# Late mode rows of a spectral mix: from waiting for them in every token tile to adding them by small row-group products in 16 of 36 tiles

## The chip, the cores and the metric

The kernel runs on one core of a Trainium2 chip. The metric is the device time of one execution in microseconds (us). The engines are TensorE (PE, with its weight load PEld), VectorE (DVE), ScalarE (ACT), GpSimd (POOL) and SyncE (SP); SP, ACT and POOL also issue DMAs, each from a queue of its own that it works off in order.

## What is computed

Two stages follow each other. First sliding-window causal attention over `q`, `k`, `v` of shape (8 batches, 8 heads, 576 tokens, 64), with a window of 64 tokens; its output `x` is (8, 576, 512). Then a spectral mix over the tokens:

```python
X = np.fft.rfft(x, axis=1)
Xr, Xi = (np.real(X[:, :n_modes]), np.imag(X[:, :n_modes]))   # 64 modes
Yr = np.einsum('bmd,mde->bme', Xr, w_r) - np.einsum('bmd,mde->bme', Xi, w_i)
Yi = np.einsum('bmd,mde->bme', Xr, w_i) + np.einsum('bmd,mde->bme', Xi, w_r)
Y[:, :n_modes] = Yr + 1j * Yi
y = np.fft.irfft(Y, n=S, axis=1)
u = x + y
return (u + np.maximum(u @ w_ch, 0.0)).astype(np.float32)
```

`w_r` and `w_i` are 64 matrices of 512 x 512 in fp32 (134 MB together, read once), `w_ch` is one.

## The kernel before

**Order of the work.** Attention and the forward transform fill `x_sb`, `x4` (x in bf16) and `XQ` (the transform of x by mode, one tile for each half of the 512 input channels). Meanwhile POOL issues the loads of `w_r` and `w_i` one after the other into rings of buffers (L156); a load converts fp32 to bf16 on the way and waits until the products that read its buffer's former contents are done. The modes are worked off in 16 groups of four (`steps`): `mode_half` (L165 to L182) multiplies four modes for one half of the channels and one of the two weights, with four 32-column groups of the PE array side by side (8 products of 512 columns). I call each such call a half-step. The loads set its pace: 2 loads of 512 KB as written, every 4.97 us. The groups 14 and 15 come before 12 and 13 (`LAST` = 12), so groups 12 and 13 are the last; their 16 rows of the 128-row spectrum (real and imaginary part of eight modes) are the **late rows**.

**What is done between half-steps.** A list `jobs` is worked off by `advance()`, a set number after each half-step. An *x job* makes x w for one token tile (four transposes, ACT copy, four products with `wch` on L591, DVE copy into `XW[i]`). A *batch job* (L654) prepares the spectrum of one batch: DVE copies `YT[:, b]` to fp32 (L657), PE turns it (L660), ACT writes `Yall[:, b]`, PE multiplies by `w_ch`, DVE writes `Zall[:, b]` (L665). `Yall` holds Y and `Zall` holds Y w_ch, each with 128 rows for each batch; batches 0 and 1 have tiles of their own (`Y0`, `Z0`, `Y1`, `Z1`). `advance()` keeps one job in flight: a job's products come after the next job's transposes. The jobs are given out so that 34 of them (26 x jobs, 8 batch jobs) are spread over the 22 half-steps before the last two, and what is left is drained there.

**The end of the loads.** Before the very last half-step, PE gets fillers (`keep_warm`, L186, products that nobody reads: 5 ahead and 4 inside), the sums of the first of the two late groups for batches 0 and 1 (`put_first`) and three products for the first tiles.

**The tail (L798 to L838).** When the last group has been added up, DVE writes it to `stg` (L612). PE turns it (L623), ACT copies it (L636), and then the late rows are made in two ways: for batches 0 and 1 directly by small products into `Y0`, `Y1`, `Z0`, `Z1` (L804, L805, L812, L830), and for all batches through `yst` and `zst`, which two DMAs on SP's queue scatter into the late rows of `Yall` (L815) and `Zall` (L824). Then 36 token tiles of 128 x 512 are finished: 32 of one batch, and 4 (`x4`) that hold the last 64 tokens of two batches. Each tile needs u = x + T Y and r = x w + T Z, and gives u + max(r, 0). Odd tiles ("by DVE", L691) take a product T Y (L697), a product of the identity with `XW` (L723), a product T Z (L697); DVE adds x (L715), ACT takes the maximum (L730), POOL adds (L731). Even tiles take one more product, the identity with x (L703); ACT copies u (L718), DVE does the rest (L733). An x4 tile needs two products T Y and two T Z. Buffers for u come in pairs from a ring of 7; PSUM banks go round in five pools (`m`, `t`, `y`, `p`, `z`). Outputs leave from SP's queue (L738), the last few also from ACT's.

Of the kernel before, what the change touches and what calls it, by code (L numbers as in the profile page):

```python
# [26 lines left out]
def kernel(  # L27
# [36 lines left out]

    consts = pool("consts")
# [4 lines left out]
    pick = consts.tile([128, 2, 24], BF16, name="pick")  # L70
# [12 lines left out]
    XQ = {0: xpool.tile([128, 3 * NJ + 2, B, NM], BF16, name="XQ0")}  # L83
    late = {}
# [80 lines left out]
    def mode_half(psm, grp, hb, ri, first, last):  # L165
        pairs = range(4 * grp, 4 * grp + 4)
        order = [(j, p) for j in range(NJ) for p in pairs]
# [3 lines left out]
        for j, p in order:  # L171
            g = p % 4
            if ending and j == 0 and g >= 2:
                keep_warm(2)
            nc.tensor.matmul(out=psm[32 * g:32 * g + 32, :],  # L175
                             lhsT=XQ[hb].rearrange("k s b m -> k (s b) m")[:, (3 * j + 1 - ri) * B:(3 * j + 5 - ri) * B, p],
# [11 lines left out]
    with tc.manual_schedule():  # L188
# [223 lines left out]
        def trig_steps():  # L412
# [5 lines left out]
            yield lambda: ve.tensor_copy(out=pick[:, :, 8:16], in_=sel.rearrange("p g (r b) -> p b (g r)", b=B)[:, 0:2])  # L418
            yield lambda: zero_xq(1, ve)

# [92 lines left out]
        Y0 = zpool.tile([128, DM], BF16, name="Y0")  # L513
        Z0 = zpool.tile([128, DM], FP32R, name="Z0")
        Y1 = zpool.tile([128, DM], BF16, name="Y1")
        Z1 = zpool.tile([128, DM], FP32R, name="Z1")
        rowpool = pool("rowpool", reuse_waits="tile")
        trpool = pool("trpool", bufs=3, reuse_waits="tile")
# [55 lines left out]

        def yrows(b):
            return (Y0, Y1)[b] if b < 2 else Yall[:, b, :]

        def zrows(b):
            return (Z0, Z1)[b] if b < 2 else Zall[:, b, :]

# [13 lines left out]
        def advance():  # L594
            if jobs:
                prepare, done = jobs.pop(0)
                pend.append((prepare(), done))
                if len(pend) < 2:
                    return
            if pend:  # L600
                tr, done = pend.pop(0)
                done(multiply(tr))
# [4 lines left out]
        def finish_group(grp, psm):  # L607
# [22 lines left out]
            def put_first():  # L630
                for b in range(2):
                    nc.tensor.matmul(out=late["first"][32 * b:32 * b + 16, :], lhsT=pick[:, b, 8 - 8 * i:24 - 8 * i],
                                     rhs=stg, start=(i == 0), stop=(i == 1), tile_position=(0, 32 * b))

            def take():
                nc.scalar.copy(out=late["tr"][:, :, 64 * i:64 * i + 64], in_=pt[:, :, 64 * i:64 * i + 64])  # L636

            def prepare():
                turn()
                if end:  # L640
                    put_y()
                    late["tr"] = Zall[:, 0, :].rearrange("p (c k) -> p c k", c=NDCH)
# [5 lines left out]
            if end:  # L648
                late[i] = turn, put_first, take, put_y
# [4 lines left out]
        def batch_job(b):  # L654
# [9 lines left out]
            def done(pz):  # L664
                nc.vector.tensor_copy(out=zrows(b), in_=pz)  # L665

            jobs.append((prepare, done))

# [9 lines left out]
        def x_jobs(pl, lo, hi):  # L678
            for i in range(lo, hi):
                def done(pz, i=i):  # L680
                    XW[i] = pl.tile([128, DM], FP32R, name=f"xw{i}")
                    nc.vector.tensor_copy(out=XW[i], in_=pz)  # L682
                jobs.append((lambda i=i: transposed(tiles[i][0]), done))

        AHEAD = 4
        pu, us, ps = {}, {}, {}
# [3 lines left out]

        def by_dve(i):  # L691
            return i % 2 == 1 and i < NT - 3
# [7 lines left out]
        def tail_x(i):  # L700
            pu[i] = bank("mmy"[i % 3])
            if not by_dve(i):
                nc.tensor.matmul(out=pu[i].rearrange("p (h e) -> p h e", h=2), lhsT=ident_bf, rhs=tiles[i][0],  # L703
                                 start=True, stop=False)

        def tail_u(i):
            if i < NT:
                if i not in pu:
                    tail_x(i)
                add_rows(pu[i], i, trigI, yrows, by_dve(i))  # L710
                if i % 2 == 0:
                    late["u"] = ringA.tile([128, 2, DM], FP32, name="ut", tag="wt")
                us[i] = late["u"][:, i % 2, :]
                if by_dve(i):
                    nc.vector.tensor_tensor(out=us[i].rearrange("p (h e) -> p h e", h=2),  # L715
                                            in0=pu[i].rearrange("p (h e) -> p h e", h=2), in1=tiles[i][0], op=ALU.add)
# [154 lines left out]
```

## Time and profile before

| what | us |
|---|---|
| three runs, median (lowest to highest) | 441.35 (441.26 to 441.49) |
| the profiled execution, its own time | 441.02 |
| span of its trace | 439.2 |
| start of the last `stg` copy (L612) | 398.01 |
| first output DMA issued (L738) | 403.05 |
| last DVE instruction of the tail (L733) ends | 434.05 |

Span and own time differ by 1.82 us that lie outside the trace. Busy shares over the span: PE 80%, DVE 50%, ACT 40%, POOL 33%. Times in the trace are us from the start of the span. A line of the timeline has start, duration, engine, line, operation, output <- inputs, shape, count, and in brackets how long the engine had been idle and what ended that.

### The profile page before, as it was taken

To read this page: it belongs to the slowest core of one execution; us is meant where nothing else is said; L and a number is where in the kernel's file an instruction comes from. 1 tells how busy PE (TensorE), PEld (TensorE's weight loads), DVE (VectorE), ACT (ScalarE), POOL (GpSimd) and SP (SyncE) were. 2 spreads that over 40 slices of the span, in tenths; PEclk is the share of its full clock that TensorE was granted. 3 is DMA by queue.
4 is the path that set the end of the run, shared out by engine and by line. 5 is a ranking of instruction groups with operands and counts; after the bars stand their busy time and mean duration, and the time that the engine had idled before them with its cause. 6 is when DMAs were issued, how large, how long until landed. Compare 5 with 4: busy or idle time off the path is not lost.

```text
span 439.2 us, 10995 instructions
## 1 busy us (share of the span) xinstructions
PE 350.0 (80%) x4728; PEld 219.5 (50%) x4728; DVE 219.9 (50%) x447; ACT 173.7 (40%) x307; POOL 143.4 (33%) x211
## 2 busy tenths in 40 slices
PE   6999999998999997986336565766778766799994
PEld 3666767676767664662113223334454433453552
DVE  8588787876776763775014111212223122345773
ACT  5666667575667663533002101111122121124662
POOL 9333323323233233223232232122232222301773
PEclk9999999999999996988559556788889689899999
DMA  8999999999999999999999999999999999992887
GB/s 205 211 211 211 212 210 211 211 211 211 212 211 212 212 210 211 211 212 211 211 258 211 211 211 211 211 211 211 212 211 211 211 211 211 212 177 67 271 305 263
DMA packets 47873, 93.45 MB, mean 213 GB/s; under 512 B 3536, under 2 KB 3664, under 8 KB 47824
## 3 DMA queue, kind: packets, MB, share of 16 engines
q0 software_dynamic: 42000, 81.73, 98.6%
q1 hardware_dynamic: 5600, 10.62, 7.2%
q8 instruction: 37, 0.61, 0.5%
q10 hardware_dynamic: 224, 0.39, 0.3%
q14 instruction: 12, 0.10, 0.1%
HBM read 163.58 MB, written 9.44 MB: 394 GB/s over the span
## 4 chain that ended last, share of the span: by engine, by line
DMA 47%; PE 41%; issue 5%; ACT 3%; DVE 3%; POOL 1%; DVEq 0%; POOLq 0%
DMA wi<-in_moe_w_i_dram 24%; DMA wr<-in_moe_w_r_dram 11%; DMA rawk<-in_k_dram 7%; PE tr L222 6%; DMA wch<-in_moe_w_ch_dram 4%; PE s L269 4%; PE pt L289 4%; PE s L261 4%; PE s L281 3%; PE psm L175 3%; PE vb L234 3%; PE o L309 2%; PE psz L591 1%; PE psm L697 1%; PE pst L723 1%
## 5 line engine op out<-in xcount | busy, mean ns | idle before, releaser
L591 PE MATMUL psz<-wch,tr 128*128 128x512 f32 x176 | 67.2, 517 | 10.9 <-DMA wch<-in_moe_w_ch_dram 10.9
L156 POOL DMA_DIRECT2D wi<-in_moe_w_i_dram x62 | 43.9, 709 | 95.7 <-PE psm L175 49.2
L682 DVE CAST xw<-psz 128x512 fp32r<-128x512 f32 x36 | 24.9, 691 | 91.4 <-PE psz L591 90.9
L156 POOL DMA_DIRECT2D wr<-in_moe_w_r_dram x53 | 37.9, 714 | 87.9 <-PE psm L175 38.0
L175 PEld LDWEIGHTS <-XQ 128*32 128x32 bf16 x512 | 24.0, 165 | 81.0 <-issue 73.6
L273 DVE TENSOR_REDUCE mx<-s 128x4 fp32r<-128x512 f32 x72 | 49.5, 687 | 26.3 <-PE s L269 26.0
L568 ACT CAST tr<-ptx 128x512 fp32r<-128x512 bf16 x36 | 21.1, 587 | 103.8 <-PE ptx L584 103.8
L175 PE MATMUL psm<-wi,XQ 128*32 128x512 bf16 x244 | 34.0, 466 | 30.6 <-DMA wi<-in_moe_w_i_dram 30.6
L591 PEld LDWEIGHTS psz<-wch,tr 128*128 128x128 f32 x176 | 40.1, 252 | 17.4 <-issue 11.2
L175 PE MATMUL psm<-wr,XQ 128*32 128x512 bf16 x212 | 29.8, 485 | 22.0 <-DMA wr<-in_moe_w_r_dram 21.3
L283 ACT ACTIVATE p<-s 128x512 bf16<-128x512 f32 x72 | 39.8, 604 | 13.0 <-PE s L281 13.0
L226 ACT COPY kT<-tr 128x576 bf16<-128x576 bf16 x32 | 23.2, 724 | 24.4 <-PE tr L222 24.4
L731 POOL TENSOR_TENSOR ut<-ut,XQ 128x512 f32<-128x512 f32 x16 | 20.5, 1284 | 28.1 <-ACT XQ L730 27.5
L292 DVE COPY pts<-pt 128x1024 bf16<-128x1024 bf16 (+1 forms) x40 | 25.2, 629 | 8.3 <-PE pt L289 7.0
L269 PE MATMUL s<-kT,qT 64*64 64x128 bf16 (+1 forms) x576 | 29.2, 221 | 0.0
L261 PE MATMUL s<-mask_t,ident_bf 128*128 128x512 bf16 x72 | 28.4, 395 | 0.9 <-ACT p L283 0.8
L226 ACT COPY qT<-tr 128x576 bf16<-128x576 bf16 x32 | 23.3, 729 | 10.7 <-PE tr L222 10.7
L269 PEld LDWEIGHTS <-qT 64*64 64x64 bf16 x576 | 17.8, 107 | 18.0 <-issue 17.5
L281 PE MATMUL s<-mx,ident_r 128*128 128x512 f32 x72 | 26.4, 438 | 0.0
L289 PE MATMUL pt<-ident_bf,p 128*128 128x128 bf16 x288 | 23.8, 223 | 1.5 <-issue 1.3
L226 ACT COPY vT<-tr 128x576 bf16<-128x576 bf16 x32 | 23.3, 728 | 4.0 <-PE tr L222 3.9
L321 DVE TENSOR_TENSOR x_sb<-o,r 128x512 bf16<-128x512 f32 x32 | 22.1, 691 | 1.1
(182 smaller groups left out, 567.2 us busy)
## 6 DMA issues: line engine op xcount, KB each, us to landing
wi<-in_moe_w_i_dram POOLq DMA_DIRECT2D x60, 512.0 KB, 15.9
wr<-in_moe_w_r_dram POOLq DMA_DIRECT2D x53, 512.0 KB, 16.3
out_dram<-ut SPq DMA_DIRECT2D x31, 256.0 KB, 2.4
rawv<-in_v_dram POOLq DMA_DIRECT2D x16, 288.0 KB, 14.4
rawk<-in_k_dram POOLq DMA_DIRECT2D x15, 288.0 KB, 15.1
rawq<-in_q_dram POOLq DMA_DIRECT2D x15, 288.0 KB, 14.1
Ypair<-in_moe_w_r_dram POOLq DMA_DIRECT2D x5, 512.0 KB, 14.9
x_sb<-in_moe_w_r_dram POOLq DMA_DIRECT2D x4, 512.0 KB, 15.2
```

The lines of the kernel that those rows point to most:

```text
L156: nc.gpsimd.dma_start(out=w[:, 0:len(ps)], in_=src[ps[0]:ps[-1] + 1, HALF * hb:HALF * hb + HALF, :].rearrange("g (p j) e -> p g j e", j=NJ))
L175: nc.tensor.matmul(out=psm[32 * g:32 * g + 32, :], lhsT=XQ[hb].rearrange("k s b m -> k (s b) m")[:, (3 * j + 1 - ri) * B:(3 * j + 5 - ri) ...
L222: nc.tensor.transpose(out=pt[ro, j, :], in_=raw[ro, TH * half + j, :], identity=ident_bf[ro, ro])
L226: nc.scalar.copy(out=to, in_=pt.rearrange("p j n -> p n j"))
L261: nc.tensor.matmul(out=s, lhsT=ident_bf, rhs=mask_t[:, mk], start=True, stop=True)
L269: nc.tensor.matmul(out=s[ro, t, lo:128], lhsT=lq, rhs=kT[ro, 64 * n - 64 + lo:64 * n + 64], start=False, stop=True, skip_group_check=True)
L273: nc.vector.tensor_reduce(out=mx, in_=s, axis=AX.X, op=ALU.max, negate=True)
L281: nc.tensor.matmul(out=s, lhsT=ident_r, rhs=mx.unsqueeze(2).to_broadcast([128, 4, 128]), start=False, stop=True, skip_group_check=True)
L283: nc.scalar.activation(out=p[:, 4 * c2:4 * c2 + 4, :], in_=s, func=ACT_F.Exp, scale=EX_SCALE)
L289: nc.tensor.transpose(out=pt[:, t, :], in_=st[u]["p"][:, t, :], identity=ident_bf)
L292: nc.vector.tensor_copy(out=ps[:, 0:nt, :], in_=pt[:, 0:nt, :])
L591: nc.tensor.matmul(out=pz, lhsT=tr[:, c, :], rhs=wch[:, c, :], start=(c == 0), stop=(c == NDCH - 1))
```

## The change

Sixteen of the 36 tiles (the four 128-token tiles of each of batches 0 to 3; `NLB` = 4) are handled in two steps.

*Under the last loads* (`early_job`): after the batch job of batch b come four early jobs. Each makes T Z with all rows of `Zall[:, b]` as they are then, the late rows being zero (`trz` and the late rows of `YT` are cleared once), and DVE adds it to `XW[i]` in place; then T Y, to which x is added: for odd c by DVE into a spare region of `XQ`, for even c by one more product (identity with x), copied by ACT over the place of x in `x_sb`. So x + T Y and x w + T Z lack only the late rows. Since `XQ` is overwritten, the columns of the last two groups are copied to `XL` beforehand and `mode_half` reads them there.

*In the tail*: the 16 late rows of batches 0 to 3 are laid on partitions 0, 32, 64 and 96 (`YL`, `ZL`, with matching copies `trigL`, `trigLr` of the late rows of the inverse table, made once by 8 small DMAs). Each of the sixteen tiles takes identity x `XW` and two products over 16 rows in one of four row groups of the array (`late_u`, `late_z`); DVE adds to `UE` (L775), ACT takes the maximum, POOL adds (L782). All other 20 tiles, the four x4 tiles among them, take the full path (`full`): four products (an x4 tile six), ACT copy, DVE. The tiles go in pairs: three pairs of the first kind ("late pairs"), then five times a full pair (the two with x4 tiles first) and a late pair, then five full pairs.

The x jobs are now given out over 16 half-steps, and the 24 batch and early jobs over the next 6, four after each. `trpool` has 2 buffers (before: 3). `Y0`, `Z0`, `Y1`, `Z1` and the direct products for batches 0 and 1 are gone. The order on the queue of SP in the changed tail is: `Yall` rows (L884), the outputs of the first two tiles, `Zall` rows (L895), then the other outputs. The diff, cut:

```diff
+    of, p0 = (XL[hb], 4 * LAST) if grp // 2 == LAST // 2 else (XQ[hb], 0)
...
+        for hb in range(2):
+            XL[hb] = zpool.tile([128, 3 * NJ + 2, B, 8], BF16, name=f"XL{hb}")
+            nc.vector.tensor_copy(out=XL[hb], in_=XQ[hb][:, :, :, 4 * LAST:4 * LAST + 8])
...
-        trpool = pool("trpool", bufs=3, reuse_waits="tile")
+        trpool = pool("trpool", bufs=2, reuse_waits="tile")
...
+        rows = slice(8 * LAST, 8 * LAST + 16)
+        YG, ZG = (64, 96, 0, 32), (0, 32, 64, 96)
...
             def put_first():
-                for b in range(2):
-                    nc.tensor.matmul(out=late["first"][32 * b:32 * b + 16, :], lhsT=pick[:, b, 8 - 8 * i:24 - 8 * i],
-                                     rhs=stg, start=(i == 0), stop=(i == 1), tile_position=(0, 32 * b))
+                nc.tensor.matmul(out=late["first"], lhsT=pick[:, 8 - 8 * i:136 - 8 * i], rhs=stg,
+                                 start=(i == 0), stop=(i == 1))
...
+            def take_first():
+                nc.scalar.copy(out=trz[:, :, :, 8 * i:8 * i + 8],
+                               in_=pt[:, :, 64 * i:64 * i + 64].rearrange("p c (r b) -> p c b r", b=B)[:, :, 0:NLB])
...
+        def early_job(b, c):
+            i = 9 * (b // 2) + 4 * (b % 2) + c
+            tokens = slice(128 * c, 128 * c + 128)
+            def done(_):
+                pz = bank("z")
+                nc.tensor.matmul(out=pz, lhsT=trigIr[:, tokens], rhs=zrows(b), start=True, stop=True)
+                nc.vector.tensor_tensor(out=XW[i], in0=pz, in1=XW[i].bitcast(FP32), op=ALU.add)
+                pu = bank("t")
+                halves = pu.rearrange("p (h e) -> p h e", h=2)
+                if c % 2:
+                    nc.tensor.matmul(out=pu, lhsT=trigI[:, tokens], rhs=yrows(b), start=True, stop=True)
+                    UE[i] = spare[2 * b + c // 2].rearrange("p (h e) -> p h e", h=2)
+                    nc.vector.tensor_tensor(out=UE[i], in0=halves, in1=tiles[i][0], op=ALU.add)
+                else:
+                    nc.tensor.matmul(out=halves, lhsT=ident_bf, rhs=tiles[i][0], start=True, stop=False)
+                    nc.tensor.matmul(out=pu, lhsT=trigI[:, tokens], rhs=yrows(b), start=False, stop=True)
+                    UE[i] = x_sb[:, :, b, c:c + 2, :].rearrange("p h c e -> p h (c e)").bitcast(FP32)
+                    nc.scalar.copy(out=UE[i], in_=halves)
...
+        def tail_xw(n):
+            for j, i in enumerate(seq[n]):
+                ps[i] = bank("zt"[n % 2 == 0])
+                nc.tensor.matmul(out=ps[i], lhsT=ident_r, rhs=XW[i], start=True, stop=False)
+        def banks_u(n):
+            for j, i in enumerate(seq[n]):
+                pu[i] = bank("m" if n % 2 == 0 else "yp"[j])
+        def late_u(n):
+            for i in seq[n]:
+                (at, b), = tiles[i][1]
+                r = slice(YG[b], YG[b] + 16)
+                nc.tensor.matmul(out=pu[i], lhsT=trigL[r, at:at + 128], rhs=YL[r], start=True, stop=True,
+                                 tile_position=(YG[b], 0))
+        def late_z(n):
+            for i in seq[n]:
+                (at, b), = tiles[i][1]
+                r = slice(ZG[b], ZG[b] + 16)
+                nc.tensor.matmul(out=ps[i], lhsT=trigLr[r, at:at + 128], rhs=ZL[r], start=False, stop=True,
+                                 tile_position=(ZG[b], 0))
...
+        def take_u(n):
+            for i in seq[n]:
+                nc.vector.tensor_tensor(out=UE[i], in0=pu[i].rearrange("p (h e) -> p h e", h=2), in1=UE[i], op=ALU.add)
+        def take_z(n):
+            ut = ringA.tile([128, 2, DM], FP32, name="ut", tag="wt")
+            for j, i in enumerate(seq[n]):
+                rt = ut[:, j].rearrange("p (h e) -> p h e", h=2)
+                nc.scalar.activation(out=ut[:, j], in_=ps[i], func=ACT_F.Relu)
+                nc.gpsimd.tensor_tensor(out=rt, in0=UE[i], in1=rt, op=ALU.add)
+                send(i, ut[:, j], n)
+        def full(n):
+            banks_u(n)
+            ut = ringA.tile([128, 2, DM], FP32, name="ut", tag="wt")
+            for j, i in enumerate(seq[n]):
+                nc.tensor.matmul(out=pu[i].rearrange("p (h e) -> p h e", h=2), lhsT=ident_bf, rhs=tiles[i][0],
+                                 start=True, stop=False)
+                add_rows(pu[i], i, trigI, yrows, False)
+                nc.scalar.copy(out=ut[:, j], in_=pu[i])
+            tail_xw(n)
+            for j, i in enumerate(seq[n]):
+                add_rows(ps[i], i, trigIr, zrows, False)
+                nc.vector.scalar_tensor_tensor(out=ut[:, j], in0=ps[i], scalar=0.0, in1=ut[:, j],
+                                               op0=ALU.max, op1=ALU.add)
+                send(i, ut[:, j], n)
...
-                    want = (half - n0) * (NT - NX0 + B) // (n1 - 2)
+                elif half <= n0 + n1 - 8:
+                    want = (half - n0) * (NT - NX0) // (n1 - 8)
+                else:
+                    want = NT - NX0 + (half - n0 - n1 + 8) * (B + 4 * NLB) // 6
...
         turn()
+        take_first()
+        put_first()
+        ZL = trpool.tile([128, NDCH, 128], FP32R, name="tr").rearrange("p c k -> p (c k)")
+        YL = stgpool.tile([128, DM], BF16, name="stg")
+        nc.vector.tensor_copy(out=YL, in_=first)
+        zl = bank("z")
+        for c in range(NDCH):
+            nc.tensor.matmul(out=zl, lhsT=trz[:, c].rearrange("p g k -> p (g k)"), rhs=wch[:, c, :],
+                             start=(c == 0), stop=(c == NDCH - 1))
+        put_y()
         take()
+        nc.vector.tensor_copy(out=ZL, in_=zl)
         yst = rowpool.tile([128, DM], BF16, name="yst")
         nc.scalar.copy(out=yst, in_=late["py"])
         nc.sync.dma_start(out=Yall[rows], in_=yst)
+        banks_u(0)
+        late_u(0)
+        take_u(0)
         pz = bank("p")
         for c in range(NDCH):
             nc.tensor.matmul(out=pz, lhsT=tr[:, c, :], rhs=wch[:, c, :], start=(c == 0), stop=(c == NDCH - 1))
         zst = trpool.tile([128, NDCH, 128], FP32R, name="tr").rearrange("p c k -> p (c k)")
+        late_z(0)
+        take_z(0)
         nc.vector.tensor_copy(out=zst, in_=pz)
         nc.sync.dma_start(out=Zall.bitcast(FP32)[rows], in_=zst.bitcast(FP32))
+        for n in range(1, len(seq)):
+            if seq[n][0] in UE:
+                tail_xw(n)
+                banks_u(n)
+                late_u(n)
+                late_z(n)
+                take_u(n)
+                take_z(n)
+            else:
+                full(n)
```

## Prediction

> **What bounds the kernel now.** I read the page's slices first, then the chain of work that ended last, then the timeline around both.
>
> ```profile
> PE   6999999998999997986336565766778766799994
> ...
> PEclk9999999999999996988559556788889689899999
> ...
> GB/s 205 211 211 211 212 210 211 211 211 211 212 211 212 212 210 211 211 212 211 211 258 211 211 211 211 211 211 211 212 211 211 211 211 211 212 177 67 271 305 263
> ```
>
> A slice is 10.98 us. For 35 slices the loads write a steady 211 GB/s: they set the time, and PE has room (6 to 8 tenths), at a clock that dips. In slices 36 and 37 the loads run out; then the outputs go, with PE full. The chain (start, duration, engine, tile, line) shows the hand-over:
>
> ```profile
> 392.09 0.67 PE psm L175 x5
> 392.76 1.19 PE psz L186 x5
> 394.26 0.67 PE pst L723 x2
> 395.16 0.58 PE psm L175 x4
> ...
> 398.01 0.70 DVE stg L612
> ...
> 432.45 0.48 DVE ut L733 x2
> ```
>
> The last two loads were issued at 382.94 and 383.5 and took a median 13.7 us, so the last landed near 397.2; its products ended at 398.0. From 405 to 432.5 the windows of 2 us show PE busy 2.00 of 2.00. So PE bounds the tail, and the change is aimed at PE there:
>
> ```profile
> 408.85 0.39 PE L703 MATMUL psm<-x_sb,ident_bf 128*128 128x512 bf16 x1
> ...
> 410.68 0.39 PE L703 MATMUL psm<-x_sb,ident_bf 128*128 128x512 bf16 x1
> ...
> 412.29 0.39 PE L703 MATMUL psy<-x_sb,ident_bf 128*128 128x512 bf16 x1
> ```
>
> Most pairs of tiles take 1.61 us (410.68 to 412.29): 7 products at 0.23. Each product of 512 columns is shown with 0.39, but they are pipelined; 0.23 is their pace. The outputs are near their own bound: the best window (424 to 426) moves 383 GB/s, the tail's mean from 416 to 432 is 310.
>
> **The change, step by step.** I keep the time axis of the run before and add shifts at the end.
>
> *1. Under the loads: +2.2 us on the end of the loads.* The 16 early jobs add 40 products (9.2 us of PE), 24 DVE additions (pace 0.61 back to back, 14.6 us) and 8 ACT copies; the x jobs move earlier. Up to 387 idle PE time hides this (idle 1.3 to 2.0 us before each second load). It stops hiding at the half-step that lands near 387.1. Its products end at 388.05. Then come 4 sets of transposes (0.25 each: a set and four L591 products take 389.16 - 387.94 = 1.22), 3 products of an early job, and 4 times 4 products (0.96): 1.0 + 0.7 + 3.84 = 5.5, to 393.6. DVE has 14 operations to give there from 385.3 (10 at 0.61, 4 at 0.42: 7.8 us), interlocked with PE by two banks each and by `trpool`'s two buffers; followed link by link that costs 0.9 more: 394.5. Before, PE was through at 391.56 and waited for the load until 392.09. Now the next half-step ends at 395.2; 5 fillers, `put_first` and two products with `XW` (8 x 0.23 and switches) at 397.3; the last half-step with its 4 fillers took 2.92 before (395.09 to 398.01): 400.2 instead of 398.0. The fillers, hidden before, are on the path now. Low end: DVE costs nothing, +1.3. High end: the clock falls at 382 as it did before, +4.2. `XL`, `trz` and the 8 small DMAs fall where DVE and SP idle (DVE waits 8.89 us at 207): nothing; uncovered, some 2 us (three operations at 0.69).
>
> *2. The first late pairs and the queue of SP: a wait of 3.5 us.* From the last sums (398.01): `stg` 0.69, turning to 399.05 (L623), `take_first` 0.26 (estimate between the rows 128x256 0.37 and 128x512 0.59 of ACT), four products to 400.5 (L808 1.11), `ZL` on DVE 0.69 to 401.25, `late_z` behind the four products L890 at about 402.6, the maximum on ACT 0.60, then POOL:
>
> ```profile
> 415.75 1.28 POOL L731 TENSOR_TENSOR ut<-ut,XQ 128x512 f32<-128x512 f32 x1 [0.33 <-ACT XQ L730]
> ```
>
> and the list of DMA issues (KB each, us to landing) has the scatter:
>
> ```profile
> Zall<-tr SPq DMA_DIRECT2D x1, 256.0 KB, 4.3
> ```
>
> POOL ends the first two tiles at 404.5 and 405.8. SP's queue holds the `Zall` scatter (L895) *behind* their outputs, so it goes out at 406.1; before, it went at 403.93, behind an output that only waited for DVE. It took 4.3 us: it lands at 410.4. PE is through the late pairs 0 to 2 and the u part of the first full pair at 406.9, and that pair's T Z reads all rows of `Zall`. PE waits 3.5 us, and every later tile is queued behind in PE's order. Before, the first read of `Zall` was at 410.9, late enough. Bounds: landing in 3.1 (the `Yall` scatter) makes 2.3; a loaded queue 4.5. POOL and SP lose nothing more by it: they are behind with pairs 1 and 2 until 410.8.
>
> *3. The clock: +1.9 us.* What such a pause does, a row of before tells:
>
> ```profile
> 372.20 0.99 PE L175 MATMUL psm<-wr,XQ 128*32 128x512 bf16 x6 [2.04 <-DMA wr<-in_moe_w_r_dram]
> ...
> 373.49 2.06 PE L591 MATMUL psz<-wch,tr 128*128 128x512 f32 x4
> ...
> 377.96 1.17 PE L591 MATMUL psz<-wch,tr 128*128 128x512 f32 x4
> ```
>
> After 2.04 us idle the same four products take 2.06 instead of 1.17; the granted clock is 0.61 and 0.54 in the next two windows of 2 us and 1.00 after 376. So a slow stretch of 3.8 us loses 1.9. Low end 0 (after 1.60 us idle at 350.7 the clock held). The Trainium skill ("TensorE: Matmul & The Clock Gate", "The HAM clock gate") has PE fall to half after an idle window of about 3.4 us, free-running; a 2.04 us gap sufficed here, and by its rule a wait of 3.5 us would only just do, so the sum would be 0 or 1.9 by chance.
>
> *4. PE's tail: -1.6 us.* A late pair is 2 products with `XW` (0.46), 2 `late_u`, 2 `late_z`. The trace has no product confined to 16 rows with all columns. Together in pairs they take 0.23 + 0.23, one after another 0.46 + 0.46. Nearest rows: 8 products of L175 in four column groups take 0.78, not 8 x 0.23 = 1.84; 8 products of L269, in quadrants with rows and columns apart, 0.41. I take together. Changing the array's division costs: at 395.09 four L175 products, two deep, take 0.59 to the next start, not 0.46, and the two full ones behind them 0.53: 0.13 + 0.07. A late pair is 0.46 + 0.46 + 0.20 = 1.12 us. The Trainium skill speaks against this part here: "Changing tiling mode (not just tile) drains the TensorE" ("TensorEngine Tiling (Array Packing)", "Key Properties"), two drains a pair; the 0.20 agrees, and without it the sum would be 1.0 us less. A full pair is 8 products (1.84), one with x4 tiles 12 (2.76). After 410.4: 4 products (0.92), 5 late pairs (5.6), one x4 pair (2.76), 8 full pairs (14.72) = 24.0, to 434.4, or 436.3 with the slow clock. PE's last product before was handed over at 432.47. Without wait and clock it would now be 430.9: -1.6. DVE (2.44 us per late and full pair), ACT (about 1.9) and POOL (2.56) keep below the 2.96 of PE there; the outputs left at 410.4 (30 tiles, 7.9 MB) need 20.6 us at 383 GB/s: no bound.
>
> *5. The end: -1.3 us.* Before, DVE ended at 434.05, 1.58 after PE, and the span 5.15 later, as outputs were still queued (2 us windows at share 1.03 to 436). Now five full pairs at 1.84 send only 285 GB/s: 1.3 and some 4.1 (landing 2.0 at the least, the rest as before).
>
> *Sum:* +2.2 + 3.5 + 1.9 - 1.6 - 1.3 = **+4.7 us**, on 441.02 of the profiled execution: **445.7**. The median of the runs, 441.35, lies 0.3 above that execution; I keep to the execution.
>
> **Rivals.**
> - *The row groups run one after another.* For: no row shows them together. Each of the five late pairs after the wait costs 0.46 more: +2.3, **448.0**.
> - *The clock holds through the wait.* For: the 1.60 us case. Against: the 2.04 us case. **443.8**.
> - *The wait for `Zall` does not come* (other side). One mechanism, the wait of PE for the late rows in `Zall`, at the first full pair, price 3.5 + 1.9. It is gone if the scatter lands within 0.8 us of its issue, or goes out 3.5 us earlier. Against: the row of 4.3, and outputs in front that wait for POOL. **440.3**, faster by 0.7.
> - *The early sums do not fit* (the change doesn't do what it says): PE at half clock from 382 to 386, as before, then late by 4.2. **447.7**.
>
> **How the numbers follow.** Forecast 0.50, row groups 0.17, clock 0.17, no wait 0.12, early sums 0.04. A measurement of this kernel tells 0.2% (0.9 us) from no change. The no-wait case is at that edge: half faster, half same (with step 1 at its low end it is 439.4); of the clock case, with step 1 at its low end and a scatter of 3.1 us (441.7), 0.02 is same. So faster 0.06, same 0.08, slower 0.86. The range reaches from the low bounds of the clock case (441.7) to 1 us above the serial row groups: 441.5 to 449.0; outside lie the no-wait case and the joint high ends.
>
> **What would show it.** Step 1: the late `stg` copy starts at 400.2, and nothing waits for a load after 393. Step 2: PE idles some 3.5 us at the first L740 product that reads `Zall`, ended by the DMA from `tr`, whose issue follows POOL's second addition. Step 3: granted clock near 0.5 in the two windows after it. Step 4: late pairs every 1.1 us of PE, with the starts of the two `late_u` closer than 0.1 us. I am wrong if PE never stops in the tail, or if `stg` starts at 398.

## The result, and the profile after

| what | before | after |
|---|---|---|
| runs, median us (lowest to highest) | 441.38 (441.26 to 441.49, 4 runs) | 448.44 (448.17 to 448.99, 4 runs) |
| profiled execution, own time, us | 441.02 | 448.99 |
| span of its trace, us | 439.2 | 447.2 |

The changed kernel is slower: ratio 1.0161, 95% interval 1.0144 to 1.0179, 7.1 us of medians. The forecast was 445.7 in a range of 441.5 to 449.0: right in sign and range, 2.7 us too low. The profiled execution of after is the slowest of its four, so its span differs from that of before by 8.0 us; the ledger below adds up to that.

The page's slices of the changed kernel (11.18 us each) show the loads as steady as before to the 35th; the loss lies behind them:

```profile
PE   6888899998999978974254565576866688796885
...
PEclk9999999999999998986569676798899899999799
...
GB/s 203 210 212 210 211 211 210 211 211 213 210 211 211 211 211 210 211 211 211 235 233 218 211 211 211 211 211 211 211 211 211 211 211 211 211 65 99 210 292 282
```

Behind the 35 slices of loads come 65, 99, 210, 292 and 282 GB/s, where before had 177, 67, 271, 305 and 263: the outputs take a slice longer to get going. In that slice, the 38th (413.7 to 424.8), the clock digit falls to 7; before, the last five slices held 9. The timeline of the same trace (start, duration, engine, line; in brackets how long the engine had been idle, and what ended that) says why:

```profile
401.31 0.69 DVE L625 CAST stg<-psm 128x512 bf16<-128x512 f32 x1 [4.58 <-PE psm L178]
...
408.13 1.58 SPq L771 DMA_DIRECT2D out_dram<-ut  x2
410.06 0.59 SPq L895 DMA_DIRECT2D Zall<-tr  x1
...
414.33 2.07 PE L740 MATMUL psz<-Zall,trigIr 128*128 128x512 f32 x4 [4.18 <-DMA Zall<-tr]
...
423.50 0.39 PE L789 MATMUL psy<-x_sb,ident_bf 128*128 128x512 bf16 x1 [1.27 <-DVE x_sb L775]
...
430.68 0.39 PE L789 MATMUL psy<-x_sb,ident_bf 128*128 128x512 bf16 x1 [1.50 <-DVE x_sb L775]
```

The late sums are copied 3.30 us later than before (398.01). SP issues the scatter of `Zall` only behind the first two outputs, and PE then stands 4.18 us for it, at the first full pair. The last two rows were not foreseen: twice more PE stands at a full pair for DVE's addition to `UE` (L775), which for even c lies over `x_sb`. The product reads another batch of `x_sb`, so no value is needed from that addition; what PE waits for is that nothing is being written in the same tile.

The windows of 2 us (span, then busy time of PE, PEld, DVE, ACT, POOL with counts, then granted clock with 1.00 for full speed, DMA share, GB/s) show the clock after the long wait:

```profile
409.00:411.00 2.00, 1.15 (x5) 0.48 (x3) 0.61 (x2) 1.37 (x3) 2.00 (x3) 1.00 0.70 261
411.00:413.00 2.00, 0.00 (x0) 0.00 (x0) 0.00 (x0) 0.00 (x0) 2.00 (x3) 0.82 0.91 160
413.00:415.00 2.00, 0.67 (x2) 0.58 (x3) 0.00 (x0) 0.00 (x0) 1.24 (x2) 0.50 0.98 331
415.00:417.00 2.00, 2.00 (x6) 1.24 (x4) 1.18 (x2) 0.00 (x0) 0.00 (x0) 0.50 0.44 165
417.00:419.00 2.00, 2.00 (x8) 0.72 (x8) 1.37 (x3) 0.98 (x2) 0.31 (x1) 0.50 0.69 151
419.00:421.00 2.00, 2.00 (x10) 1.38 (x9) 0.15 (x2) 1.27 (x3) 2.00 (x2) 0.98 0.62 142
```

PE works at half clock from 414.33 to about 419: four products in 2.07 us instead of 1.2. From 414.33 to the second pair of products with `XW` (419.60) it is 5.27 us; the same products take 3.15 at full clock in the first experiment below (410.36 to 413.51), 2.1 us less.

**The ledger**, from trace to trace. PE's last product ends at 432.87 before and 442.67 after. From `stg` to there before takes 34.86 us, after 41.36.

| term | us | from |
|---|---|---|
| `stg` later | +3.30 | 401.31 - 398.01 |
| wait for `Zall` | +4.18 | row at 414.33 |
| half clock behind it | +2.1 | 5.27 - 3.15 |
| two waits for `x_sb` | +2.77 | rows at 423.50 and 430.68 |
| PE's own work in the tail, as what is left | -2.55 | 41.36 - 34.86 - 4.18 - 2.1 - 2.77 |
| from PE's last product to the end of the span | -1.80 | (447.2 - 442.67) - (439.2 - 432.87) |
| sum | +8.0 | 447.2 - 439.2 |

### The profile page after: what moved, and what is told of

The parts are those of the page before. It is cut to its first block, busy times and chain, and to the rows that moved or that the text cites. A ratio compares the mean times of both kernels' runs of the same rounds, so it can differ in the third digit from the quotient of the medians.

```text
span 447.2 us, 11052 instructions
## 1 busy us (share of the span) xinstructions
PE 337.8 (76%) x4720; PEld 214.0 (48%) x4765; DVE 234.9 (53%) x476; ACT 176.8 (40%) x315; POOL 142.9 (32%) x211
## 5 line engine op out<-in xcount | busy, mean ns | idle before, releaser
L604 PE MATMUL psz<-wch,tr 128*128 128x512 f32 x176 | 59.1, 466 | 11.0 <-DMA wch<-in_moe_w_ch_dram 11.0
L178 PEld LDWEIGHTS <-XQ 128*32 128x32 bf16 x448 | 20.7, 166 | 77.0 <-issue 69.0
L178 PE MATMUL psm<-wi,XQ 128*32 128x512 bf16 x212 | 28.3, 461 | 31.1 <-DMA wi<-in_moe_w_i_dram 30.8
L604 PEld LDWEIGHTS psz<-wch,tr 128*128 128x128 f32 x176 | 34.9, 220 | 17.5 <-issue 11.5
L178 PE MATMUL psm<-wr,XQ 128*32 128x512 bf16 x180 | 25.1, 482 | 22.8 <-DMA wr<-in_moe_w_r_dram 22.8
L623 DVE TENSOR_TENSOR stg<-psm,Ypair 128x512 bf16<-128x512 f32 x10 | 6.9, 689 | 32.4 <-PE psm L178 32.4
L225 PE MATMUL tr<-ident_bf,rawk 64*64 64x64 bf16 x576 | 15.4, 196 | 6.2 <-DMA rawk<-in_k_dram 4.8
```

The source lines that it names most:

```text
L178: nc.tensor.matmul(out=psm[32 * g:32 * g + 32, :], lhsT=of.rearrange("k s b m -> k (s b) m")[:, (3 * j + 1 - ri) * B:(3 * j + 5 - ri) * B, ...
L604: nc.tensor.matmul(out=pz, lhsT=tr[:, c, :], rhs=wch[:, c, :], start=(c == 0), stop=(c == NDCH - 1))
```

## The experiments

Theories at this point: *(T1)* the `Zall` wait comes from the place of its DMA behind outputs that wait for POOL, and the slow clock from that wait; *(T2)* the `x_sb` waits come from the order of the tiles and add to the first; *(T3)* the fillers, no longer hidden, make `stg` late; *(T4)* the row groups do run side by side. Against these stand the rivals in the expectations, above all that something behind PE ends the tail. The first four kernels have 4 runs each, beside 7 of the kernel before (441.25). All ratios are to the kernel before on the same chip; the chips differ by up to 0.14 us in its median.

### The late rows of Z first

```diff
         late_z(0)
-        take_z(0)
         nc.vector.tensor_copy(out=zst, in_=pz)
         nc.sync.dma_start(out=Zall.bitcast(FP32)[rows], in_=zst.bitcast(FP32))
+        take_z(0)
```

> The Zall scatter is issued before the outputs of the first late pair instead of behind them; nothing else moves. Theory (the queue of SP holds it behind POOL's additions): it goes out at about 406.5 on the axis of the changed kernel's trace, 3.5 us earlier, lands at 410.8, PE (there at 410.2) waits under 1 us instead of 4.2, and the clock does not fall (2.1 us less): 5.6 us gained, about 442.8 us. Rival A (the scatter is slow because of the outputs beside it, not late): landing takes longer by what it starts earlier, about 448. Rival B (the pause goes, but the outputs' own bound takes its place): about 3 us gained, 445.5.

Measured: **443.08** (442.91 to 443.38), ratio 1.0040 (1.0025 to 1.0055): 5.4 us less than the changed kernel. In its timeline the scatter goes out ahead of the outputs:

```profile
406.08 0.57 SPq L894 DMA_DIRECT2D Zall<-tr  x1
407.71 8.65 SPq L771 DMA_DIRECT2D out_dram<-ut  x9
...
410.36 1.20 PE L740 MATMUL psz<-Zall,trigIr 128*128 128x512 f32 x4 [0.61 <-DMA Zall<-tr]
```

The wait is 0.61 us instead of 4.18, the four products behind it take 1.20 instead of 2.07, and the granted clock stays at 1.00. From `stg` (400.89) to PE's last product (436.58) it is 35.69 us, 5.67 less than in the changed kernel: the wait's 3.57 and the clock's 2.1. The queue's order costs both, which confirms T1. The two waits for `x_sb` are still there (1.27 and 1.51 us), and the clock holds through them.

### The late pairs over x_sb first

```diff
-        AA = [(18 * k // 2 + c, 18 * k // 2 + 4 + c) for k in range(NLB // 2) for c in range(4)]
+        AA = [(18 * k // 2 + c, 18 * k // 2 + 4 + c) for cs in ((0, 2), (1, 3)) for k in range(NLB // 2) for c in cs]
```

> The late pairs whose sums lie over x_sb come first in the tail, so that the pairs behind them are late pairs or x4 pairs, which do not read x_sb. Theory (a full pair's read of x_sb waits for DVE's write of a late pair over another part of x_sb; 1.27 and 1.50 us of PE in the changed kernel): both waits go, 2.8 us gained, about 445.7 us. Rival (at these places PE is held by DVE and ACT being behind after the slow clock, whatever the tile): the waits move to other names, time unchanged at 448.4.

Measured: **445.53** (445.31 to 445.82), ratio 1.0096 (1.0079 to 1.0113): 2.9 us less. No product waits for `x_sb` any more; the wait for `Zall` is 4.15 us. The two waits were an effect of the order alone: the first part of T2 holds. But not all of the 2.9 us is theirs. In this trace the clock is slow for a shorter time behind the wait for `Zall` (414.10 to 417.05), so that the products there lose 1.3 us instead of 2.1; some 0.8 of the gain is that.

### No fillers

```diff
-        for _ in range(n):
+        for _ in range(0):
             nc.tensor.matmul(out=late["warm"], ...
```

> The nine products of the filler that nobody reads are left out (the sums of the output are complete). Theory (they are on the path since PE comes late to the last half-steps): the late stg copy starts 2 to 2.7 us earlier, about 446.0 us. Rival A (they still hide behind the last loads): stg moves by under 0.5 us, 448.2. Rival B (without them the clock falls before the tail): stg earlier, but the first part of the tail slower, 448 or more.

Measured: **446.49** (446.36 to 446.72), ratio 1.0117 (1.0102 to 1.0132): 2.0 us less. `stg` starts at 398.34 instead of 401.31, and the clock before the tail stays at 1.00 without fillers, so nothing was lost by leaving them out. The wait for `Zall` stays (4.18 us) and after it the clock is slow for longer (411.4 to 417.5): the products there lose 2.8 us instead of 2.1, and from `stg` to PE's last product it is 42.05 us instead of 41.36. That is where 0.7 of the 3.0 us went; and 0.3 of them is a load stream that was that much ahead at 230 us already in this trace. T3 holds.

### Late pairs of one batch

Two tiles of a late pair are now of the same batch, so that their two `late_u` share one row group, and their two `late_z` another.

```diff
-        AA = [(18 * k // 2 + c, 18 * k // 2 + 4 + c) for k in range(NLB // 2) for c in range(4)]
+        AA = [(18 * k // 2 + 4 * j + c, 18 * k // 2 + 4 * j + c + 2) for k in range(NLB // 2) for j in range(2) for c in (0, 1)]
```

> Each late pair takes two tiles of the same batch, so that its two u products share one row group and its two w products another. Theory (products in different row groups run side by side: four in 0.43 us in the changed kernel): two run one after the other, the four take 0.43 + 0.2; only the five late pairs behind the wait for Zall count: +1.0 us, 449.4. Rival (the row groups do not matter, the four products are short for another reason): unchanged within 0.3 us.

Measured: **451.7** (447.74 to 452.53), ratio 1.0217 (1.0172 to 1.0262). The time is a poor witness, since its runs lie 4.8 us apart; the timeline is a good one. The changed kernel, one late pair (with the first product of the next):

```profile
406.04 0.73 PE L746 MATMUL psz<-xw,ident_r 128*128 128x512 f32 x2
406.70 0.39 PE L756 MATMUL psy<-stg,trigL 16*128 16x512 bf16 x1
406.70 0.38 PE L756 MATMUL psp<-stg,trigL 16*128 16x512 bf16 x1
406.70 0.50 PE L763 MATMUL psz<-tr,trigLr 16*128 16x512 f32 x2
407.13 0.73 PE L746 MATMUL pst<-xw,ident_r 128*128 128x512 f32 x2
```

and the kernel with pairs of one batch:

```profile
406.44 0.73 PE L746 MATMUL psz<-xw,ident_r 128*128 128x512 f32 x2
407.10 0.38 PE L756 MATMUL psy<-stg,trigL 16*128 16x512 bf16 x1
407.11 0.50 PE L763 MATMUL psz<-tr,trigLr 16*128 16x512 f32 x1
407.33 0.37 PE L756 MATMUL psp<-stg,trigL 16*128 16x512 bf16 x1
407.44 0.39 PE L763 MATMUL psz<-tr,trigLr 16*128 16x512 f32 x1
407.76 0.74 PE L746 MATMUL pst<-xw,ident_r 128*128 128x512 f32 x2
```

In the first, all four products of 16 rows start in the same instant and a pair takes 1.09 us; in the second, the two of one row group follow each other by 0.23 or 0.33 us, while the other row group's run beside them, and a pair takes 1.32. T4 holds, and the rival of the prediction that row groups run one after another falls. The expected 449.4 counted the five pairs behind the wait for `Zall`, 1.15 us at 0.23; the three ahead of it only shorten that wait (3.43). The rest is in the trace: the half clock lasted from 414.5 to 423.5, 4.3 us longer than in the changed kernel, and its products lose 4.1 us instead of 2.1. With `Zall` landing 0.2 later and the waits of the full pairs 0.5 shorter, that makes the 2.9 us by which PE's last product is late. Why the slow stretch is longer here, and whether it gives the spread of the runs, was not tried.

### Both repairs of the tail; then without fillers

The next four kernels were run on one chip, beside 24 runs of the kernel before (441.38). The edits are the first two above; the second kernel adds the third.

> The two repairs of the tail together: the late rows of Z go ahead of the first outputs on SP's queue, and the late pairs that use x_sb go first in the order. Theory (the wait for Zall with its slow clock, and the wait for x_sb, are two separate waits in PE's order, so that their prices add): alone the first brought 448.44 to 443.08 and the second 448.44 to 445.53, so together 448.44 - 5.36 - 2.91 = 440.2, just under the kernel before (441.38); PE does not stop in the tail. Rival (without the waits something behind PE, the outputs or POOL, ends the run, so that part of the second gain is lost): 441.3 or more, and the span ends over 4.5 us after PE's last product.

Measured: **442.91** (442.71 to 443.10, 5 runs), ratio 1.0034 (1.0022 to 1.0046). The expectation is missed by 2.7 us, and the rival holds: with the `Zall` wait at 0.61, removing the `x_sb` waits gains only 0.2 (0.3 by the ratios). PE does what the theory said: its last product ends at 434.00, 2.6 us before that of the kernel with Z first (436.58). But both spans are 441.1. The windows of 4 us show what fills the gap:

```profile
420.00:424.00 4.00, 4.00 (x20) 2.63 (x20) 3.36 (x7) 3.30 (x7) 3.46 (x3) 1.00 0.94 303
424.00:428.00 4.00, 4.00 (x21) 2.17 (x21) 3.62 (x6) 2.96 (x7) 3.72 (x4) 1.00 1.04 384
428.00:432.00 4.00, 3.95 (x18) 2.28 (x17) 2.58 (x4) 2.49 (x5) 0.39 (x1) 1.00 1.03 380
432.00:436.00 4.00, 2.01 (x9) 1.06 (x8) 2.58 (x4) 1.07 (x2) 0.00 (x0) 1.00 1.03 382
436.00:440.00 4.00, 0.00 (x0) 0.00 (x0) 0.00 (x0) 0.00 (x0) 0.00 (x0) 0.61 0.82 307
```

From 424 on the outputs move 380 to 384 GB/s with a DMA share above 1, past the end of all engines at 435.2: the span ends 5.9 us after DVE, against 3.3 in the changed kernel. The waits had been hiding an output bound. And the sum was too hopeful by some 0.8: the 2.91 held that much of the slow clock, which the other repair takes away by itself.

> Both repairs of the tail, and no filler products. Theory (the fillers are on the path, since the early jobs made PE late for the last loads): alone their removal brought 448.44 to 446.49, so 440.2 - 1.95 = 438.3, and the last stg copy starts near 399.3. Rival (the fillers keep the clock up for the tail, which this version needs because its wait no longer hides it): granted clock under 0.9 in the first windows of the tail, and 440 or more.

Measured: **440.24** (440.03 to 440.64, 8 runs), ratio 0.9974 (0.9964 to 0.9984): faster than the kernel before, by 1.1 us. The expected 438.3 is missed because it started from 440.2; the step itself is 2.7 us instead of 1.95; alone it had lost 0.7 to the longer slow clock, and no slow clock follows here. `stg` starts at 398.49. The rival falls: the clock is 1.00 throughout the tail.

### Early sums behind the next batch

```diff
                             batch_job(b)
-                            if b < NLB:
+                            if 1 <= b <= NLB:
                                 for c in (1, 0, 3, 2):
-                                    early_job(b, c)
+                                    early_job(b - 1, c)
```

> As the kernel with both repairs and no fillers, and the early sums of a batch are queued behind the next batch's products instead of right behind its own. Theory (part of the backlog under the last loads is PE waiting for DVE's copy to Zall, 0.78 us at each batch, before its early sums can start): with another job between, these waits go; the backlog at the end of the loads shrinks by about 0.8 us, 437.5. Rival (DVE, which has some 12 us of additions and copies to do there, sets the pace, and PE's waits only move): 438.3, as without it, and other waits for DVE of the same sum.

Measured: **440.34** (439.65 to 444.11, 12 runs), ratio 0.9994 (0.9974 to 1.0013): no gain against 440.24. Three of the 12 runs, at 442.95 to 444.11, pull the ratio up; what set them apart is open. Neither theory is quite it. PE reaches the last half-step 0.65 us earlier (396.51 instead of 397.16), so the backlog did shrink. But there it now waits for the last load:

```profile
396.51 0.86 PE L178 MATMUL psm<-wi,XL 128*32 128x512 bf16 x6
398.09 0.59 PE L178 MATMUL psm<-wi,XL 128*32 128x512 bf16 x2 [0.72 <-DMA wi<-in_moe_w_i_dram]
```

Without fillers there is no backlog left to win: the last load decides again, as before the change.

### The late tables without the small DMAs

```diff
-                for g in range(4):
-                    nc.sync.dma_start(out=trigL[32 * g:32 * g + 16], in_=trigI[rows, 0:512])
-                    nc.sync.dma_start(out=trigLr.bitcast(FP32)[32 * g:32 * g + 16], in_=trigIr.bitcast(FP32)[rows, 0:512])
+                nc.tensor.matmul(out=p1[0:16], lhsT=ident_bf[:, rows], rhs=trigI[:, 0:512], start=True, stop=True)
+                for g in range(4):
+                    nc.scalar.copy(out=trigL[32 * g:32 * g + 16], in_=p1[0:16])
+                nc.tensor.matmul(out=p2[0:16], lhsT=ident_r[:, rows], rhs=trigIr[:, 0:512], start=True, stop=True)
+                for g in range(4):
+                    nc.vector.tensor_copy(out=trigLr[32 * g:32 * g + 16], in_=p2[0:16])
```

> As the kernel with both repairs and no fillers, and trigL and trigLr are made by two selection products and eight copies of 16 rows instead of by the eight small DMAs. Theory (the eight DMAs, 192 KB, take their bytes' time from the load stream, 192 KB at 211 GB/s = 0.9 us, of which 0.5 us showed as lag of the loads): the lag between 230 and 246 us is gone, 437.8 (0.5 under the same kernel with the DMAs). Rival (the lag of 0.5 us is from something else at that place, or is made up later): 438.3, no difference.

Measured: **440.25** (439.90 to 440.88, 9 runs), ratio 0.9974 (0.9965 to 0.9984). The load stream did what the theory said, the time did not. The issues of two loads ahead of and behind the place, in the changed kernel:

```profile
230.44 0.71 POOL L158 DMA_DIRECT2D wr<-in_moe_w_r_dram  x1 [1.66 <-DMA wr<-in_moe_w_r_dram]
...
263.40 0.71 POOL L158 DMA_DIRECT2D wr<-in_moe_w_r_dram  x1 [1.80 <-DMA wr<-in_moe_w_r_dram]
```

and without the small DMAs:

```profile
230.22 0.72 POOL L158 DMA_DIRECT2D wr<-in_moe_w_r_dram  x1 [1.65 <-DMA wr<-in_moe_w_r_dram]
...
262.60 0.71 POOL L158 DMA_DIRECT2D wr<-in_moe_w_r_dram  x1 [1.82 <-DMA wr<-in_moe_w_r_dram]
```

They lie 32.96 us apart with the DMAs and 32.38 without: eight DMAs of 192 KB together cost the loads 0.58 us between these two. Over all twelve traces the same distance is 32.96 to 33.05 in the eight kernels with these DMAs and 32.38 to 32.59 in the four without (before: 32.49), so some 0.5 us. `stg` starts at 397.84, 0.65 earlier, and PE's last product ends at 430.62 instead of 431.28. The span is not shorter (438.7, against 438.3; the profiled execution is the slowest of nine here and the fastest of eight there, and the medians are equal), because the outputs end it: they move 379 to 382 GB/s from 420 to 436, to the end of the span but for 2.7 us.

### DVE takes a share from POOL, with the new order and with the old

What paces the outputs between 404 and 420? The candidate is POOL, which makes the first six tiles at 1.28 us each.

```diff
+                if j and n < 3:
+                    nc.vector.scalar_tensor_tensor(out=rt, in0=ps[i].rearrange("p (h e) -> p h e", h=2), scalar=0.0, in1=UE[i],
+                                                   op0=ALU.max, op1=ALU.add)
+                else:
                     nc.scalar.activation(out=ut[:, j], in_=ps[i], func=ACT_F.Relu)
                     nc.gpsimd.tensor_tensor(out=rt, in0=UE[i], in1=rt, op=ALU.add)
```

> As the kernel without small DMAs (both repairs, no fillers, 440.25), and of each of the first three late pairs the second tile's maximum and addition are one operation of DVE (0.70 us) instead of one of ACT and one of POOL (1.28 us). Theory (with the waits of PE gone, the outputs bound the tail: from 420 us on they move 380 to 384 GB/s without a break, and the time was lost between 404 and 420, where they moved 215 on the mean because POOL makes the first six tiles at 1.28 us each): POOL has three tiles fewer, 3.8 us, the outputs start the full stretch some 2 us earlier, 438.2. Rival (PE's and DVE's order sets the end, and DVE, which gets three operations more, passes its delay on): 440.2 or more.

Measured, beside 15 runs of the kernel before (441.39): **438.89** (438.64 to 439.16, 5 runs), ratio 0.9941 (0.9928 to 0.9953). The windows of 4 us without DVE's share (440.25):

```profile
404.00:408.00 4.00, 3.39 (x17) 1.69 (x16) 2.13 (x4) 2.90 (x6) 4.00 (x4) 1.00 0.82 200
408.00:412.00 4.00, 4.00 (x21) 2.46 (x20) 2.66 (x5) 2.06 (x4) 4.00 (x4) 1.00 0.61 225
412.00:416.00 4.00, 3.95 (x21) 2.12 (x21) 3.46 (x6) 2.09 (x5) 3.49 (x4) 1.00 0.66 159
```

and with it:

```profile
404.00:408.00 4.00, 3.37 (x17) 1.72 (x16) 3.48 (x6) 2.10 (x4) 3.09 (x3) 1.00 0.96 256
408.00:412.00 4.00, 4.00 (x21) 2.43 (x20) 2.68 (x5) 2.05 (x4) 1.89 (x2) 1.00 0.99 306
412.00:416.00 4.00, 3.95 (x21) 2.13 (x21) 3.46 (x6) 2.11 (x5) 2.83 (x3) 1.00 0.66 193
```

POOL is no longer busy 4.00 of 4.00, the outputs move 200 to 256 and 225 to 306 GB/s, and PE's columns are the same. PE's last product ends at 430.59 against 430.62, the span at 437.1 against 438.7: all of the gain is outputs that left earlier. The theory holds, at 1.4 us instead of 2. It is the fastest kernel of this study, 2.5 us below the kernel before.

The second kernel keeps DVE's share and goes back to the changed kernel's order of tiles.

> As the kernel with DVE's share (no small DMAs, no fillers, late rows of Z first), but with the order of tiles of the changed kernel, so that PE waits twice for the additions over x_sb. Theory (the outputs' bound had swallowed the price of these waits: 442.91 with the new order against 443.08 without): where the outputs start earlier, the waits show again, up to 2.8 us over the same kernel with the new order, 440 to 441. Rival (the waits cost nothing wherever the late rows of Z come in time): the same time as the kernel with the new order, 438.2.

Measured: **440.85** (440.73 to 441.12, 11 runs), ratio 0.9988 (0.9979 to 0.9997), 2.0 us above the new order. The waits are back, 1.26 and 1.51 us:

```profile
414.46 0.39 PE L793 MATMUL psy<-x_sb,ident_bf 128*128 128x512 bf16 x1 [1.26 <-DVE x_sb L775]
...
421.63 0.39 PE L793 MATMUL psy<-x_sb,ident_bf 128*128 128x512 bf16 x1 [1.51 <-DVE x_sb L775]
```

So the same 2.8 us of PE were worth some 2.1 in the changed kernel (2.9 less the 0.8 of the clock in its trace), 0.2 where POOL held the outputs back, and 2.0 where it no longer did. This settles what happened to the missing 2.7 us: some 0.8 had been counted twice, and the other 1.9 the outputs swallowed. The prices of waits add only up to the next bound.

## Why the prediction was right, and where it was off

The mechanism it named carried the change: the scatter behind the outputs on SP's queue, the wait, the clock, and a PE saving too small to pay for them. Its sum missed 2.4 us of the 7.1 of the medians (3.3 of the 8.0 between the traces); point by point:

*Step 1, +2.2 (measured +3.30).* The range (+1.3 to +4.2) holds it, but two of its parts went otherwise. The 8 small DMAs were put at nothing, as SP idles; their 192 KB pass through the DMA engines that the loads keep busy (DMA share 1.1): some 0.5 us. A lag of 0.36 at 230 us is there ahead of them; the traces of one and the same load program differ as much (230.09 to 230.44), so it belongs to no step. What is left, 3.30 - 0.36 - 0.47 (the growth from 230 to 263 in this trace) = 2.47, is the backlog with the fillers, forecast 2.2 by the link-by-link sum. The fall of the clock at 382, the high end, did not come: 1.00 from 378 to 402.

*Step 2, wait of 3.5 (measured 4.18).* Right in place, cause and releaser. With Z first the wait is 0.61, not nothing: the rival "the wait does not come" needed the scatter 3.5 us earlier, and it went out 3.98 us earlier (406.08 against 410.06), of which 0.42 is the earlier `stg` of that run (400.89); 3.57 of a wait of 4.18 leave 0.61.

*Step 3, clock, +1.9 (measured 2.1).* Right in kind; that the size fits is partly luck, since waits of 3.4 to 4.2 us lost 1.3, 2.1, 2.8 and 4.1 us in the four traces that have them. The prediction had weighed the Trainium skill ("TensorE: Matmul & The Clock Gate", "The HAM clock gate"): half rate after an idle window of about 3.4 us, free-running. The trace agrees that a wait of this size does it, and with a window of that length that runs freely: the falls and returns lie whole multiples of 3.41 us apart (last section). It does not agree that a whole window must be idle: the clock fell at 412.26, some 2.1 us into the idle time that began at 410.15 (3.45 us into it in the kernel without fillers), and here the measurement decides. The waits of 1.26 to 1.51 us never cost clock here.

*Step 4, PE's tail, -1.6 (measured -2.55).* Row groups side by side, as taken: four products in the same instant. Of the two rows it took this from, that of L175 (512 columns) bears on it; that of L269 does not, as its products have 128 columns, and eight of them one after another would take 8 x 0.23 / 4 = 0.46 us (an estimate), hardly more than the 0.41 seen. The pitch was 1.09, not 1.12, and a late pair with a full pair takes 2.80 in the kernel with both repairs (415.59, 418.38, 421.18 in its chain), not 2.96: 5 x 0.16 = 0.8 of the 0.95. The Trainium skill gives 3.07 times for four row tiles of 32 rows ("TensorE: Matmul & The Clock Gate", "Measured speedup vs the span model"); here four of 16 rows take 0.43 us with both changes of tiling, against 4 x 0.23 one after another, 2.1 times. By the prediction's rows 0.20 of the 0.43 are the changes of tiling, which is more than the difference.

*Missing: +2.77.* The step that failed is in step 4, "after 410.4" PE was given nothing but products in a row. The listing of what the late pairs write was not carried to the reads of the full pairs between them: L775 writes `UE` in `x_sb`, DVE adds there for the late pair just ahead (1.28 us) while PE is ready to go on, and L789 reads `x_sb`. The diff shows it (`UE[i] = x_sb[...]`); the trace of before, where nothing writes `x_sb` in the tail, could not. It is the term that took the result from 445.7 to near the upper bound. That the range still held it is luck: its upper bound had been set for row groups one after another, which did not happen.

*Step 5, the end, -1.3 (measured -1.80).* Right in kind: PE's waits thinned the outputs, so fewer were queued at the end. Its other side was not said: this end part grows back (5.9 us behind DVE with both repairs) as soon as PE is made faster. "No bound" in step 4 compared the mean need of the outputs with their peak rate; POOL's pace at the start of the tail, seen in step 2 ("behind with pairs 1 and 2 until 410.8"), was counted as no loss.

*Rivals.* Row groups in series: fell. Clock holds: fell; the four products behind the long wait took 2.07 or 2.08 us in all four traces that have it. No wait: made by hand, 443.08 instead of 440.3; the waits for `x_sb` are as large as the difference, and the other errors (`stg` +0.7, a wait of 0.6, PE's own work -0.95, the end -0.5) nearly cancel. The early sums did fit, at a clock of 1.00.

**Still open:** why the kernel with pairs of one batch spreads over 4.8 us, why three runs of the kernel with early sums behind the next batch took 2.6 to 3.8 us more than its median, and what else holds the outputs at 193 GB/s between 412 and 416 in the fastest kernel.

## What to carry to other kernels

Where a DMA that feeds the next stage shares a queue with outputs that wait for a slow engine, put it ahead: the order of issue cost 5.4 us here, 2.1 of them through the clock that fell in the wait. When scratch results are laid over a tensor that others still read, list every later reader, and order the writers first. And before adding up the gains of several repairs, look at what is behind the engine that you relieve: the same wait was worth 2.0 or 0.2 us, depending on whether the outputs behind it were the bound. A gain measured next to another stall may hold a part of that stall: 0.8 of the 2.9 us here.

## What the hardware showed that was not expected

Eight DMAs of 16 and 32 KB between two tables on the chip delay a saturated load stream by some 0.5 us (0.58 between the two traces shown), more than half of what their 192 KB take at its 211 GB/s (0.9 us).

The half clock that follows a long wait does not last a fixed time after work resumes, and yet it is not arbitrary. If the clock is at 1.00 or 0.50 at any instant, the means of windows of 0.5 us (0.76 for 412.0 to 412.5 in the changed kernel) give the moments at which it fell and rose:

| kernel | PE idle from | clock falls | PE resumes | full clock again | from fall to full | cost |
|---|---|---|---|---|---|---|
| changed | 410.15 | 412.26 | 414.33 | 419.09 | 6.83 | 2.1 |
| late pairs over x_sb first | 409.95 | 413.64 | 414.10 | 417.05 | 3.41 | 1.3 |
| no fillers | 407.19 | 410.65 | 411.37 | 417.48 | 6.83 | 2.8 |
| pairs of one batch | 411.07 | 413.28 | 414.50 | 423.52 | 10.24 | 4.1 |
| before, first case | 370.16 | 372.43 | 372.20 | 375.85 | 3.42 | |
| before, second case | 380.12 | 382.67 | 382.15 | 386.09 | 3.42 | |

The slow stretches are 2, 1, 2 and 3 times 3.41 us, and one time in both cases of before. The two falls in the trace of before lie 10.24 us apart, three times 3.41 again. So the clock changes here on a grid of 3.41 us that does not start with the wait, and one and the same kind of wait costs 1.3 to 4.1 us. What decides between one and three steps is open: in the kernel with pairs of one batch PE was busy in the whole step from 416.69 to 420.10, and the clock stayed at 0.50 for another. In these cases idle stretches of 2.03 us and more brought a fall (the two of before stand 0.4 us behind another of 0.55); those of 1.26 to 1.60 us did not.

And the fillers that were to keep the clock up were not needed: without them it was 1.00 in every window from 404 to the end of PE's work once the wait for `Zall` was down to 0.6 us.
